# The state's products of a linear-attention layer as two half-width matmuls side by side on TensorE

## The chip, the cores and the metric

The kernel runs on one core of one Trainium2 chip, as one launch. The metric is the device time of that launch in microseconds, taken over several runs. Beside the runs there is one profiled execution with a trace of every instruction. TensorE (PE) does matmuls and, overlapped with them, loads of the stationary operand (PEld); VectorE (DVE), ScalarE (ACT) and GpSimd (POOL) do the elementwise work; SyncE (SP) issues the DMAs.

## The reference

The network is two layers, with the same weights, on x of 2048 tokens by 576 features. Each layer is a linear attention block followed by a block of 64 small experts. The change touches the attention alone:

```python
qkv = (layernorm(x) @ wqkv)          # q, k, v: 32 heads of 18 features
phi = lambda t: jnp.where(t > 0, t + 1, jnp.exp(t)) + 1e-6
pq, pk = phi(q), phi(k)
kv = jnp.einsum("bhsd,bhse->bhde", pk, v)      # the state: 18 x 18 a head, summed over all tokens
z = jnp.einsum("bhsd->bhd", pk)                # the sum of pk over all tokens
num = jnp.einsum("bhqd,bhde->bhqe", pq, kv)
den = jnp.einsum("bhqd,bhd->bhq", pq, z)[..., None] + 1e-6
x = x + (num / den) @ wo                       # heads put side by side again
```

The expert block takes, for each of 32 query heads, the best of 8 keys twice, and adds gelu(x . u[e]) v[e] of the expert that the pair names.

## The kernel before

Tokens are cut into NT = 16 tiles of 128. Each layer has a front over all tiles (transposes `front_T`; k, v and q by `product`; `phi`; then `front_state`), a short stage that turns the state into a folded output matrix (`state_mask`, `state_sum`, `state_fold`), and a back over all tiles (`back_scale`, `back_oT`, `back_out`, then the experts' `exp_...`). Products that need f32 accuracy are made of split operands in f32r, three passes each (`passes`, `product`).

The state is accumulated over the 16 tiles in one PSUM tile, `kva`. `front_state` (lines 275 to 286) makes five f32 matmuls a tile: for each of four chunks of 7 heads, HC = 126 columns, the stationary operand is 126 columns of v and a column of ones, 127 in all, and the moving operand is the same chunk's 126 columns of phi(k); the fifth chunk has 4 heads, 73 by 72. Each product thus holds every pair of heads in its chunk, and only the 18 x 18 blocks on the diagonal are wanted. The row of the ones is the sum z. v is put into `v5` by three ACT copies in `front_v` (lines 244 to 248), two of 252 columns and one of 72, around columns of ones that were set once in `small_loads`.

When the last tile is in, `state_mask` (lines 301 to 308) multiplies the chunks on DVE by a mask of the diagonal blocks into `kvb`, the row of sums included; `state_sum` (line 310) spreads that row over all 128 partitions with five matmuls whose stationary operand `pick` selects it, and ACT copies the result to `zb` (line 317). `state_fold` (line 327) multiplies each chunk's masked block by its rows of wo, which `wo_load` (line 289) loads, and ACT and DVE split the product into `ohi` and `olo` for `back_out`.

The order of the work on PE, ACT, DVE and POOL is written out: `in_order` makes each engine keep the program's order within a block, and the order is given by the loop from line 724 for tiles 2 to 12 of layer 0 (tiles 2 to 9 have the fold of w_q, `fold_mm`, right behind `front_state`), by the strings given to `play`, and by `step2`. In the strings, `st` is `front_state`, `mk` is `state_mask`, `zs` is `state_sum`, `M` is `state_fold`, `wl` is `wo_load`. In layer 0 `mk0.0 zs0.0x2` comes right after `st0.14 st0.15`; in layer 1 the order is `st1.15 mk1.0 M1.1 zs1.0 ...`, and `st1.11 st1.12` are adjacent. SP issues DMAs in the order of the program, each after the waits for its tile.

`fold_mm` (line 542) is the one place where matmuls use a part of the array's columns: the stationary operand has 32 columns, and the output goes to one of four strips of 32 partitions, `p[32 * j:32 * j + 32]`.

Of the kernel before, what the change touches and what calls it, by code (L numbers as in the profile page):

```python
# [11 lines left out]
F32 = mybir.dt.float32  # L12
# [3 lines left out]
AF = mybir.ActivationFunctionType  # L16
ALU = mybir.AluOpType
# [5 lines left out]
P = 128  # L23
NT = S // P
DK, E, NE = 128, 8, 64
HC = 7 * DH
# [9 lines left out]
NB = 5  # L36
# [21 lines left out]
def network(ctx, tc, x_in, wqkv, wo, wq_t, k_t, u_t, v2, c_mask, c_mask4, c_ident, c_code, c_code1, c_scale, c_shift, out):  # L58
    nc = tc.nc

    cp = ctx.enter_context(tc.tile_pool(name="cp", bufs=1))
# [4 lines left out]
    def psum(name):  # L66
        return ps.tile([P, 1024], F32, tag="ps", name=name)

    def halves(t):
        return t.rearrange("p (b c) -> p b c", b=2)[:, :, :HALF]  # L70


    ident = cp.tile([P, P], F32, name="ident")
    mask = cp.tile([HC + 1, HC + 72], F32, name="mask")
    pick = cp.tile([HC + 1, 2 * P], F32, name="pick")
    code_w = cp.tile([P, 512], BF16, name="code_w")
    shift = cp.tile([P, 64], I32, name="shift")
    mhalf = cp.tile([P, 1], F32, name="mhalf")
# [9 lines left out]
    slo = cp.tile([P, 4, 512], F32R, name="slo")  # L88
    vmix = cp.tile([P, D], F32R, name="vmix")

    kvb = cp.tile([HC + 1, 4 * HC + P], F32, name="kvb")
    zb = cp.tile([P, D], F32, name="zb")
    junk = cp.tile([P, D], BF16, name="junk")
    v5 = [cp.tile([P, 4 * (HC + 1) + 73], F32, name=f"v5_{i}") for i in range(2)]

    hl_d = [dr.tile([P, 2, NB, P], F32, name=f"hl_d{t}") for t in range(NT)]
    pq_d = [[dr.tile([P, D], F32, name=f"pq_d{l}_{t}") for t in range(NT)] for l in range(2)]
# [107 lines left out]
    def product(tt, hi, lo, cols, n, cut=HALF, rem=REM, by_block=False):  # L205

        o = psum(f"pp{n}")
        todo = sorted(passes(rem), key=lambda p: p[1]) if by_block else passes(rem)
        for i, (a, b, w) in enumerate(todo):
            wb = hi[:, b] if w == "hi" else lo[:, blocks(rem)[b][1]]  # L210
            for c0, c1, at in ((0, cut, 0), (cut, D, 512)):
                nc.tensor.matmul(o[:, at:at + c1 - c0], tt[a == "lo"][:, b, :], wb[:, cols + c0:cols + c1],  # L212
                                 start=(i == 0), stop=(i == len(todo) - 1))
        return o
# [24 lines left out]
    def front_v(l, t):  # L239
        v = product(tt["f", l, t], whi, wlo, 2 * D, f"v{l}_{t}", cut=2 * HC)  # L240
        yield
        vt = v5[t % 2]
        w = HC + 1
        for c, x in ((0, v[:, :2 * HC]), (2, v[:, 512:512 + 2 * HC])):
            nc.scalar.activation(vt[:, c * w:(c + 2) * w].rearrange("p (c e) -> p c e", c=2)[:, :, :HC],  # L245
                                 x.rearrange("p (c e) -> p c e", c=2), AF.Copy)
        yield
        nc.scalar.activation(vt[:, 4 * w:4 * w + 72], v[:, 512 + 2 * HC:512 + 2 * HC + 72], AF.Copy)

    def front_q(l, t):  # L250
        q = product(tt["f", l, t], whi, wlo, 0, f"q{l}_{t}")
# [23 lines left out]
    def front_state(l, t):  # L275
        fk, vt = tt.pop(("fk", l, t)), v5[t % 2]
        if t == 0:
            kva[l] = psum(f"kva{l}")
        a = kva[l]
        w = HC + 1  # L280

        for c in range(4):
            nc.tensor.matmul(a[:w, c * HC:(c + 1) * HC], vt[:, c * w:(c + 1) * w], fk[:, c * HC:(c + 1) * HC],
                             start=(t == 0 and c == 0), stop=(t == NT - 1), skip_group_check=True)
        nc.tensor.matmul(a[:73, 512:512 + 72], vt[:, 4 * w:4 * w + 73], fk[:, 4 * HC:],
                         start=(t == 0), stop=(t == NT - 1), skip_group_check=True)


    def wo_load(l, t):
        tiles = wob[l] = []  # L290
        for c, tag in enumerate(("x1", "x1", "x1", "x1", "x2")):
            st = wk.tile([P, D], F32, tag=tag, name=f"wob{c}", bufs=BUFS[tag])
            n = HC if c < 4 else 72
            nc.sync.dma_start(st[:n], wo[c * HC:c * HC + n, :])
            tiles.append(st)
        yield

    def chunk(c):
        return slice(c * HC, c * HC + (HC if c < 4 else 72))

    def state_mask(l, t):
        a = kva.pop(l)
        w = HC + 1
        for c in range(4):
            nc.vector.tensor_tensor(kvb[:, chunk(c)], a[:w, c * HC:(c + 1) * HC], mask[:, :HC], op=ALU.mult)
        nc.vector.tensor_tensor(kvb[:73, chunk(4)], a[:73, 512:584], mask[:73, HC:], op=ALU.mult)
        at = chunk(4).start
        nc.vector.tensor_copy(kvb[:72, at + 72:at + P], kvb[:72, at + 16:at + 72])

    def state_sum(l, t):  # L310

        z = psum(f"z{l}")
        for c in range(4):
            nc.tensor.matmul(z[:, 8 + c * HC:8 + (c + 1) * HC], pick[:, :P], kvb[:, chunk(c)], start=True, stop=True)
        nc.tensor.matmul(z[:, 512:584], pick[:73, P:], kvb[:73, chunk(4)], start=True, stop=True)
        yield
        nc.scalar.activation(zb, z[:, 8:584], AF.Copy)

# [8 lines left out]
    def state_fold(l, b):  # L327

        m = psum(f"m{l}_{b}")
        n, c = (HC, HC) if b < 4 else (72, P)  # L330
        for h in range(2):
            nc.tensor.matmul(m[:c, h * 512:h * 512 + HALF], kvb[:n, b * HC:b * HC + c], wob[l][b][:n, h * HALF:(h + 1) * HALF],
                             start=True, stop=True)
        yield

        def part(x, rows):
            return x[rows].rearrange("p (b c) -> p b c", b=2)

        src = halves(m)
        hi, lo = (part(x[:, b], slice(c)) for x in (ohi, olo))  # L340
        nc.scalar.activation(hi, src[:c], AF.Copy)
        if b < 4:
            nc.vector.tensor_tensor(lo, src[:c], hi.bitcast(F32), op=ALU.subtract)
            return

        nc.vector.tensor_tensor(lo[96:112], src[:16], hi[:16].bitcast(F32), op=ALU.subtract)
        nc.vector.tensor_tensor(hi[64:], src[64:], hi[64:].bitcast(F32), op=ALU.subtract)
        nc.scalar.activation(lo[:72], src[:72], AF.Copy)
        nc.scalar.activation(hi[64:72], src[64:72], AF.Copy)
# [246 lines left out]
    def small_loads():  # L596
        for t in v5:
            nc.gpsimd.memset(t, 1.0)
        nc.gpsimd.memset(kpad, 0.0)
        nc.sync.dma_start(kraw, k_t)  # L600
        nc.gpsimd.tensor_tensor(kpad[:, :, 25:32], kraw[:, :, 1:], kraw[:, :, :1].to_broadcast([P, 2, E - 1]),
                                op=ALU.subtract)
        nc.gpsimd.memset(olo[:, 4].bitcast(F32), 0.0)

        nc.gpsimd.memset(mask, 1.0)
        nc.sync.dma_start(mask[:HC, :HC], c_mask[:, 7:])
        nc.sync.dma_start(mask[:72, HC:], c_mask[:72, 7:79])
        nc.gpsimd.tensor_copy(pick[:, :P], ident[:HC + 1, HC:HC + 1].to_broadcast([HC + 1, P]))
        nc.gpsimd.tensor_copy(pick[:, P:], ident[:HC + 1, 72:73].to_broadcast([HC + 1, P]))
        nc.sync.dma_start(code_w, c_code)  # L610
        nc.sync.dma_start(shift, c_shift)

# [43 lines left out]
    keep, rl, lq, ldx, ldq = front_keep, late_load, late_q, back_x, back_pq  # L656
    fl, ln, lv, sv = first_load, first_ln, load_vu, split_vu
    k, v, q, fT, st = front_k, front_v, front_q, front_T, front_state
    wl, mk, zs, M = wo_load, state_mask, state_sum, state_fold
    ld, num, oT, O = back_load, back_scale, back_oT, back_out  # L660
    S, sel, gel, po = exp_scores, exp_select, exp_gelu, exp_out
# [31 lines left out]
    with in_order(*ALL):  # L693
# [17 lines left out]
        first_load(0, 2)  # L711
        wq_in = load_weight(wqkv, 0, REM, "w")
        small_loads()
        first_load(0, 3)
        run(0, (k, 1), (v, 0, 1))
# [135 lines left out]
```

## Time and profile before

| what | value |
|---|---|
| median of 3 runs | 755.47 us (755.28 to 756.19) |
| the profiled execution's own time | 754.99 us |
| its span, first to last instruction | 753.2 us |
| mean granted TensorE clock | 0.999 |
| state matmuls (lines 283 and 285) | 320 records, 37.4 us of PE busy time |

Busy time of a group is the union of its instructions, which overlap their neighbours; a mean duration in ns is that of one instruction from start to end. What a matmul holds PE for is read from the start of one to the start of the next. In a line of the timeline the columns are the start in us, the length in us, the engine, the line of the kernel, the operation, out<-in by the program's names, rows * columns of the array in use, the partitions and elements of the output, and the count.

### The profile page before, as it was taken

Reading aid. Unit: us, or ns where it says so; the run is one execution under the profiler, and the core shown is the slowest. Engines: PE = TensorE matmul, PEld = TensorE weight load, DVE = VectorE, ACT = ScalarE, POOL = GpSimd, SP = SyncE. Lnnn points to the kernel's source line nnn. Section 1 sums busy time; section 2 is a strip of 40 time slices with the busy share of each in tenths; the row PEclk is TensorE's granted clock in tenths of the full one; section 3 lists DMA queues with packets and bytes.
Section 4 is the critical chain, followed back from the end, with each engine's and each line's share of the span. In section 5 each row is a group of like instructions: output and inputs, shape, how many; then the busy total and the mean of one; then the engine's idle time right before and its main releaser. Section 6 shows DMA issues by size and latency. Waiting matters only on the chain. (4 is left out here: it accounts for less than half of the span.)

```text
span 753.2 us, 13998 instructions
## 1 busy us (share of the span) xinstructions
PE 735.4 (98%) x5356; PEld 692.9 (92%) x5356; DVE 459.0 (61%) x1008; ACT 289.0 (38%) x586; POOL 197.1 (26%) x540
## 2 busy tenths in 40 slices
PE   7999999999999999999999999999999999999995
PEld 5999989999998989999999999999999999999984
DVE  5532342324246887666666666464366899899986
ACT  5422232232333544444444444353233333444343
POOL 2110001000002543333333333130033334533431
PEclk9999999999999999999999999999999999999999
DMA  9737446641111322322232212221734323121101
GB/s 272 248 100 243 162 169 220 220 119 49 48 63 32 111 84 82 98 84 83 87 103 105 88 67 76 90 72 51 187 86 118 103 83 114 32 84 44 48 33 63
DMA packets 52267, 79.48 MB, mean 106 GB/s; under 512 B 5480, under 2 KB 22376, under 8 KB 52200
## 3 DMA queue, kind: packets, MB, share of 16 engines
q1 hardware_dynamic: 52200, 78.59, 32.0%
q8 instruction: 42, 0.69, 0.4%
q14 instruction: 25, 0.20, 0.1%
HBM read 55.01 MB, written 23.56 MB: 104 GB/s over the span
## 5 line engine op out<-in xcount | busy, mean ns | idle before, releaser
L219 DVE TENSOR_SCALAR ek<-ek 128x576 f32<-128x576 f32 x32 | 14.7, 459 | 83.6 <-ACT ek L218 83.6
L212 PE MATMUL ppk<-whi,thif 128*128 128x288 f32 x320 | 50.2, 301 | 1.9 <-ACT thif L102 1.9
L402 PE MATMUL ppo<-ohi,thio 126*128 126x288 f32 (+1 forms) x320 | 50.7, 300 | 0.1
L212 PEld LDWEIGHTS ppk<-whi,thif 128*128 128x128 f32 x320 | 44.2, 188 | 5.9 <-issue 3.3
L163 POOL TENSOR_SCALAR rsf<-mvf 128x1 f32<-128x1 f32 x16 | 3.1, 192 | 175.7 <-DVE mvf L161 175.6
L212 PE MATMUL ppk<-whi,tlof 128*128 128x288 f32 x320 | 48.7, 296 | 0.2 <-DVE tlof L103 0.2
L219 DVE TENSOR_SCALAR eq<-eq 128x576 f32<-128x576 f32 x32 | 15.6, 488 | 54.2 <-ACT eq L218 54.2
L212 PE MATMUL ppv<-whi,thif 128*128 128x252 f32 x320 | 48.1, 296 | 0.1
L212 PE MATMUL ppv<-whi,tlof 128*128 128x252 f32 x320 | 47.6, 295 | 0.0
L187 ACT ACTIVATE yb<-x,rsb 128x640 f32<-128x640 f32 x32 | 29.5, 923 | 43.4 <-POOL rsb L180 43.3
L433 PE MATMUL pps<-shi,thib 128*128 128x512 f32 x160 | 44.0, 405 | 1.9 <-ACT thib L102 1.9
L402 PEld LDWEIGHTS ppo<-ohi,thio 126*128 126x128 f32 (+1 forms) x320 | 44.8, 189 | 0.9 <-DVE eq L221 0.3
L212 PEld LDWEIGHTS ppk<-whi,tlof 128*128 128x128 f32 x320 | 44.6, 188 | 0.5 <-DVE tlof L103 0.5
L212 PEld LDWEIGHTS ppv<-whi,tlof 128*128 128x128 f32 x320 | 44.7, 188 | 0.0
L212 PEld LDWEIGHTS ppv<-whi,thif 128*128 128x128 f32 x320 | 44.3, 188 | 0.4 <-ACT thif L102 0.3
L173 ACT ACTIVATE junk<-x,mb 128x576 bf16<-128x576 f32 x32 | 24.7, 771 | 49.7 <-POOL mb L172 46.4
L433 PE MATMUL pps<-shi,tlob 128*128 128x512 f32 x160 | 42.4, 395 | 0.0
L245 ACT ACTIVATE v<-ppv 128x252 f32<-128x252 f32 x64 | 20.9, 380 | 55.0 <-PE ppv L212 55.0
L218 ACT ACTIVATE eq<-ppq 128x576 f32<-128x576 f32 x32 | 20.7, 647 | 52.1 <-PE ppq L212 52.1
L212 PE MATMUL ppq<-whi 128*128 128x288 f32 x260 | 39.9, 300 | 0.6 <-DVE eq L221 0.6
L402 PE MATMUL ppo<-ohi,tloo 126*128 126x288 f32 x256 | 40.3, 295 | 0.0
L402 PE MATMUL ppo<-olo,thio 126*128 126x288 f32 x256 | 40.3, 296 | 0.0
(156 smaller groups left out, 1797.7 us busy)
## 6 DMA issues: line engine op xcount, KB each, us to landing
fold<-in_wq_t SPq DMA_DIRECT2D x64, 288.0 KB, 5.3
whi<-hl_d SPq DMA_DIRECT2D x26, 320.0 KB, 3.9
pq_d<-eq SPq DMA_DIRECT2D x19, 288.0 KB, 2.1
pq<-pq_d SPq DMA_DIRECT2D x19, 288.0 KB, 2.8
xf<-in_x SPq DMA_DIRECT2D x16, 288.0 KB, 5.6
x<-in_x SPq DMA_DIRECT2D x16, 288.0 KB, 2.8
x_d<-x SPq DMA_DIRECT2D x16, 288.0 KB, 3.0
x<-x_d SPq DMA_DIRECT2D x16, 288.0 KB, 2.8
```

The source lines that it names most:

```text
L163: nc.gpsimd.tensor_scalar(rs[:, 0:1], mv[:, 1:2], EPS_LN, 1.0, op0=ALU.add, op1=ALU.mult)
L173: nc.scalar.activation(junk, xt, AF.Square, bias=m[:, 0:1], accum_out=m[:, 1:2])
L187: nc.scalar.activation(y, x2, AF.Identity, scale=rs[:, 0:1], bias=rs[:, 1:2])
L212: nc.tensor.matmul(o[:, at:at + c1 - c0], tt[a == "lo"][:, b, :], wb[:, cols + c0:cols + c1], start=(i == 0), stop=(i == len(todo) - 1))
L218: nc.scalar.activation(e.rearrange("p (b c) -> p b c", b=2), halves(p), AF.Exp)
L219: nc.vector.tensor_scalar(e, e, 1.0, EPS, op0=ALU.min, op1=ALU.add)
L245: nc.scalar.activation(vt[:, c * w:(c + 2) * w].rearrange("p (c e) -> p c e", c=2)[:, :, :HC], x.rearrange("p (c e) -> p c e", c=2), AF.Copy)
L402: nc.tensor.matmul(p[:, h * 512:h * 512 + HALF], hl[a][:r, b], w[:r, h * HALF:(h + 1) * HALF], start=(i == 0), stop=(i == len(todo) - 1))
L433: nc.tensor.matmul(p[:, :512], hl[a == "lo"][:, b, :], shi[:, b] if w == "hi" else slo[:, blocks(REM)[b][1]], start=(i == 0), stop=(i == l ...
```

## The change

The state's products are made in two halves of the array's columns. A chunk of 126 columns of v is cut into two of 63, each with a column of ones (64 stationary columns), and the second half's output goes to partitions 64 to 127 of the same PSUM columns. Each half is multiplied by only those 72 columns of phi(k) that hold its 4 heads: columns 0 to 71 of the chunk for the first half and 54 to 125 for the second. (The middle head lies in both.) The last chunk is cut into two of 36 by 36. So a tile has ten matmuls of 64 stationary and 72 or 36 moving columns in place of five of 127 or 73 by 126 or 72.

The rest follows from the layout: `v5` has ten slots of 64 columns; `kvb` has 128 rows, with a row that is zero at 63 and 127, and is cleared once; wo's rows are loaded in two pieces a chunk; the masks are made by two DVE operations over four chunks each and two for the last chunk; the sums are read from a copy of the state, `zc`, which ACT makes, by four matmuls in place of five; `state_fold` contracts 127 rows (100 for the last chunk) in place of 126 (72).

```diff
-    mask = cp.tile([HC + 1, HC + 72], F32, name="mask")
-    pick = cp.tile([HC + 1, 2 * P], F32, name="pick")
+    mask = cp.tile([P, 72 + 36], F32, name="mask")
+    pick = cp.tile([P, 2, P], F32, name="pick")
+    zc = cp.tile([P, 4 * 72 + 36], F32, name="zc")
...
-    v5 = [cp.tile([P, 4 * (HC + 1) + 73], F32, name=f"v5_{i}") for i in range(2)]
+    v5 = [cp.tile([P, 10, 64], F32, name=f"v5_{i}") for i in range(2)]
...
-        for c, x in ((0, v[:, :2 * HC]), (2, v[:, 512:512 + 2 * HC])):
-            nc.scalar.activation(vt[:, c * w:(c + 2) * w].rearrange("p (c e) -> p c e", c=2)[:, :, :HC],
-                                 x.rearrange("p (c e) -> p c e", c=2), AF.Copy)
-        yield
-        nc.scalar.activation(vt[:, 4 * w:4 * w + 72], v[:, 512 + 2 * HC:512 + 2 * HC + 72], AF.Copy)
+        for c, x in ((0, v[:, :2 * HC]), (4, v[:, 512:512 + 2 * HC])):
+            nc.scalar.activation(vt[:, c:c + 4, :63], x.rearrange("p (c e) -> p c e", c=4), AF.Copy)
+        yield
+        nc.scalar.activation(vt[:, 8:, :36], v[:, 512 + 2 * HC:512 + 2 * HC + 72].rearrange("p (c e) -> p c e", c=2), AF.Copy)
...
-        for c in range(4):
-            nc.tensor.matmul(a[:w, c * HC:(c + 1) * HC], vt[:, c * w:(c + 1) * w], fk[:, c * HC:(c + 1) * HC],
-                             start=(t == 0 and c == 0), stop=(t == NT - 1), skip_group_check=True)
-        nc.tensor.matmul(a[:73, 512:512 + 72], vt[:, 4 * w:4 * w + 73], fk[:, 4 * HC:],
-                         start=(t == 0), stop=(t == NT - 1), skip_group_check=True)
+        for c in range(NB):
+            n, at = (72, 54) if c < 4 else (36, 36)
+            for h in range(2):
+                f0 = c * HC + h * at
+                nc.tensor.matmul(a[64 * h:64 * h + 64, c * 72:c * 72 + n], vt[:, 2 * c + h], fk[:, f0:f0 + n],
+                                 start=(t == 0 and c == 0), stop=(t == NT - 1), skip_group_check=True)
...
-            n = HC if c < 4 else 72
-            nc.sync.dma_start(st[:n], wo[c * HC:c * HC + n, :])
+            r, n = (63, 63) if c < 4 else (36, 36)
+            nc.sync.dma_start(st[:64], wo[c * HC:c * HC + 64, :])
+            nc.sync.dma_start(st[64:64 + n], wo[c * HC + r:c * HC + r + n, :])
...
-        for c in range(4):
-            nc.vector.tensor_tensor(kvb[:, chunk(c)], a[:w, c * HC:(c + 1) * HC], mask[:, :HC], op=ALU.mult)
-        nc.vector.tensor_tensor(kvb[:73, chunk(4)], a[:73, 512:584], mask[:73, HC:], op=ALU.mult)
+        nc.scalar.activation(zc, a[:, :4 * 72 + 36], AF.Copy)
+        for h in range(2):
+            rows = slice(64 * h, 64 * h + 64)
+            nc.vector.tensor_tensor(kvb[rows, :4 * HC].rearrange("p (c e) -> p c e", c=4)[:, :, 54 * h:54 * h + 72],
+                                    a[rows, :4 * 72].rearrange("p (c e) -> p c e", c=4),
+                                    mask[rows, :72].unsqueeze(1).to_broadcast([64, 4, 72]), op=ALU.mult)
         at = chunk(4).start
-        nc.vector.tensor_copy(kvb[:72, at + 72:at + P], kvb[:72, at + 16:at + 72])
+        for h in range(2):
+            rows = slice(64 * h, 64 * h + 64)
+            nc.vector.tensor_tensor(kvb[rows, at + 36 * h:at + 36 * h + 36], a[rows, 4 * 72:4 * 72 + 36], mask[rows, 72:], op=ALU.mult)
+        nc.vector.tensor_copy(kvb[:, at + 72:at + P], kvb[:, at + 16:at + 72])
...
-        for c in range(4):
-            nc.tensor.matmul(z[:, 8 + c * HC:8 + (c + 1) * HC], pick[:, :P], kvb[:, chunk(c)], start=True, stop=True)
-        nc.tensor.matmul(z[:, 512:584], pick[:73, P:], kvb[:73, chunk(4)], start=True, stop=True)
+        zm, sm = (x.rearrange("p (c e) -> p c e", c=4) for x in (z[:, 8:512], zc[:, :4 * 72]))
+        for h in range(2):
+            nc.tensor.matmul(zm[:, :, 72 * h:72 + 54 * h], pick[:, h], sm[:, :, 18 * h:], start=True, stop=True)
+            nc.tensor.matmul(z[:, 512 + 36 * h:548 + 36 * h], pick[:, h], zc[:, 4 * 72:], start=True, stop=True)
...
-        n, c = (HC, HC) if b < 4 else (72, P)
+        n, c = (HC + 1, HC) if b < 4 else (100, P)
...
-        nc.gpsimd.memset(mask, 1.0)
-        nc.sync.dma_start(mask[:HC, :HC], c_mask[:, 7:])
-        nc.sync.dma_start(mask[:72, HC:], c_mask[:72, 7:79])
-        nc.gpsimd.tensor_copy(pick[:, :P], ident[:HC + 1, HC:HC + 1].to_broadcast([HC + 1, P]))
-        nc.gpsimd.tensor_copy(pick[:, P:], ident[:HC + 1, 72:73].to_broadcast([HC + 1, P]))
+        nc.gpsimd.memset(kvb, 0.0)
+        nc.gpsimd.memset(mask, 0.0)
+        nc.sync.dma_start(mask[:63, :72], c_mask[:63, 7:79])
+        nc.sync.dma_start(mask[64:127, :72], c_mask[63:, 61:])
+        for r in (0, 64):
+            nc.sync.dma_start(mask[r:r + 36, 72:], c_mask[:36, 7:43])
+        for h in range(2):
+            nc.gpsimd.tensor_copy(pick[:, h], ident[:, 64 * h + 63:64 * h + 64].to_broadcast([P, P]))
```

More of the change, by code (lines that the diff above doesn't have):

```diff
@@ L89, in network @@
     vmix = cp.tile([P, D], F32R, name="vmix")
-    kvb = cp.tile([HC + 1, 4 * HC + P], F32, name="kvb")
+    kvb = cp.tile([P, 4 * HC + P], F32, name="kvb")
     zb = cp.tile([P, D], F32, name="zb")
     junk = cp.tile([P, D], BF16, name="junk")
-    v5 = [cp.tile([P, 4 * (HC + 1) + 73], F32, name=f"v5_{i}") for i in range(2)]
+    v5 = [cp.tile([P, 10, 64], F32, name=f"v5_{i}") for i in range(2)]
     hl_d = [dr.tile([P, 2, NB, P], F32, name=f"hl_d{t}") for t in range(NT)]
@@ L242, in front_v @@
         vt = v5[t % 2]
-        w = HC + 1
-        for c, x in ((0, v[:, :2 * HC]), (2, v[:, 512:512 + 2 * HC])):
-            nc.scalar.activation(vt[:, c * w:(c + 2) * w].rearrange("p (c e) -> p c e", c=2)[:, :, :HC],
-                                 x.rearrange("p (c e) -> p c e", c=2), AF.Copy)
+        for c, x in ((0, v[:, :2 * HC]), (4, v[:, 512:512 + 2 * HC])):
+            nc.scalar.activation(vt[:, c:c + 4, :63], x.rearrange("p (c e) -> p c e", c=4), AF.Copy)
         yield
-        nc.scalar.activation(vt[:, 4 * w:4 * w + 72], v[:, 512 + 2 * HC:512 + 2 * HC + 72], AF.Copy)
+        nc.scalar.activation(vt[:, 8:, :36], v[:, 512 + 2 * HC:512 + 2 * HC + 72].rearrange("p (c e) -> p c e", c=2), AF.Copy)
     def front_q(l, t):
@@ L279, in front_state @@
         a = kva[l]
-        w = HC + 1
-        for c in range(4):
-            nc.tensor.matmul(a[:w, c * HC:(c + 1) * HC], vt[:, c * w:(c + 1) * w], fk[:, c * HC:(c + 1) * HC],
-                             start=(t == 0 and c == 0), stop=(t == NT - 1), skip_group_check=True)
-        nc.tensor.matmul(a[:73, 512:512 + 72], vt[:, 4 * w:4 * w + 73], fk[:, 4 * HC:],
-                         start=(t == 0), stop=(t == NT - 1), skip_group_check=True)
+        for c in range(NB):
[4 more added lines that the diff above has]
+                                 start=(t == 0 and c == 0), stop=(t == NT - 1), skip_group_check=True)
     def wo_load(l, t):
@@ L302, in state_mask @@
         a = kva.pop(l)
-        w = HC + 1
-        for c in range(4):
-            nc.vector.tensor_tensor(kvb[:, chunk(c)], a[:w, c * HC:(c + 1) * HC], mask[:, :HC], op=ALU.mult)
-        nc.vector.tensor_tensor(kvb[:73, chunk(4)], a[:73, 512:584], mask[:73, HC:], op=ALU.mult)
+        nc.scalar.activation(zc, a[:, :4 * 72 + 36], AF.Copy)
[4 more added lines that the diff above has]
+                                    mask[rows, :72].unsqueeze(1).to_broadcast([64, 4, 72]), op=ALU.mult)
         at = chunk(4).start
-        nc.vector.tensor_copy(kvb[:72, at + 72:at + P], kvb[:72, at + 16:at + 72])
+        for h in range(2):
+            rows = slice(64 * h, 64 * h + 64)
+            nc.vector.tensor_tensor(kvb[rows, at + 36 * h:at + 36 * h + 36], a[rows, 4 * 72:4 * 72 + 36], mask[rows, 72:], op=ALU.mult)
+        nc.vector.tensor_copy(kvb[:, at + 72:at + P], kvb[:, at + 16:at + 72])
     def state_sum(l, t):
         z = psum(f"z{l}")
-        for c in range(4):
-            nc.tensor.matmul(z[:, 8 + c * HC:8 + (c + 1) * HC], pick[:, :P], kvb[:, chunk(c)], start=True, stop=True)
-        nc.tensor.matmul(z[:, 512:584], pick[:73, P:], kvb[:73, chunk(4)], start=True, stop=True)
+        zm, sm = (x.rearrange("p (c e) -> p c e", c=4) for x in (z[:, 8:512], zc[:, :4 * 72]))
+        for h in range(2):
+            nc.tensor.matmul(zm[:, :, 72 * h:72 + 54 * h], pick[:, h], sm[:, :, 18 * h:], start=True, stop=True)
+            nc.tensor.matmul(z[:, 512 + 36 * h:548 + 36 * h], pick[:, h], zc[:, 4 * 72:], start=True, stop=True)
         yield
```

## The prediction

> **What bounds the kernel now.** I read the page first, for the bound.
>
> ```profile
> span 753.2 us, 13998 instructions
> PE 735.4 (98%) x5356; PEld 692.9 (92%) x5356; DVE 459.0 (61%) x1008; ACT 289.0 (38%) x586; POOL 197.1 (26%) x540
> ```
>
> PE (matmuls) is busy for 98% of the span, and no other engine passes 61%. The state's own matmuls lie in two stretches, so the table of windows came next.
>
> ```profile
> core 0: us, PE busy (x) PEld busy (x) DVE busy (x) ACT busy (x) POOL busy (x), PEclk, DMA share, GB/s
> 20.00:230.00 210.00, 209.28 (x1743) 200.12 (x1742) 72.93 (x151) 62.69 (x144) 16.14 (x47) 1.00 0.43 145
> 270.00:540.00 270.00, 268.42 (x1934) 258.05 (x1932) 165.15 (x376) 116.20 (x240) 79.34 (x231) 1.00 0.28 91
> 640.00:753.20 113.20, 104.55 (x662) 94.19 (x660) 99.17 (x244) 45.53 (x91) 42.68 (x122) 0.99 0.15 51
> ```
>
> From 20 to 230 us (layer 0's fronts) and from 270 to 540 us (layer 1's), PE stands idle for 0.7 and 1.6 us in all, at the full clock. The stage without a PE bound, the tail from 640 us, holds no state matmul. So a microsecond taken from the state's place in PE's queue is a microsecond of the span, nearly one for one, and one added is lost the same way. The groups by line, shapes kept apart, give the rates.
>
> ```profile
> L283 PE MATMUL kva<-ek,v 128*127 128x126 f32 x256 | 33.5, 274 | 0.0
> L285 PE MATMUL kva<-ek,v 128*73 128x72 f32 x64 | 9.3, 228 | 0.0
> L283 PEld LDWEIGHTS kva<-ek,v 128*127 128x127 f32 x256 | 31.1, 190 | 0.0
> L285 PEld LDWEIGHTS kva<-ek,v 128*73 128x73 f32 x64 | 8.1, 145 | 0.0
> L550 PEld LDWEIGHTS fold_ps<-fold,kpad 128*32 128x32 f32 x256 | 8.7, 109 | 5.5
> L212 PEld LDWEIGHTS ppv<-whi,tlof 128*128 128x128 f32 x320 | 44.7, 188 | 0.0
> L197 PEld LDWEIGHTS ptb<-ident,yb 128*128 128x128 f32 x160 | 18.8, 140 | 1.9 <-ACT yb L187 1.7
> ```
>
> An f32 matmul of the program makes two records, each a weight load and a matmul: 256 records are 16 tiles, 2 layers, 4 chunks, twice. A duration has a constant part that overlaps the next record; what queues is the part that grows with columns. Matmul: (274 - 228) / (126 - 72) = 0.85 ns per moving column. Load: (190 - 145) / (127 - 73) = 0.83 ns per stationary column. So a record of L283 needs 107 ns of matmul and 105 ns of load, side by side, and one of L285 61 and 61. A load of 128 columns takes 107 ns; a transpose's is 48 ns shorter (140 against 188), 59 ns.
>
> The one place where the kernel already uses part of the array's width is the fold of w_q (L550, 32 columns). The timeline of PE around it, and of PEld at its start, shows all that the sum needs.
>
> ```profile
> 109.94 1.05 PE L283 MATMUL kva<-ek,v 128*127 128x126 f32 x8
> 110.82 0.29 PE L285 MATMUL kva<-ek,v 128*73 128x72 f32 x2
> 111.04 2.18 PE L550 MATMUL fold_ps<-fold,kpad 128*32 128x320 f32 x32
> 113.16 0.40 PE L212 MATMUL ppk<-whi,thif 128*128 128x288 f32 x1
> ...
> 110.88 0.23 PE L285 MATMUL kva<-ek,v 128*73 128x72 f32 x1
> ...
> 112.85 0.38 PE L550 MATMUL fold_ps<-fold,kpad 128*32 128x256 f32 x1
> ...
> 111.04 0.18 PEld L550 LDWEIGHTS fold_ps<-fold,kpad 128*32 128x32 f32 x8
> ```
>
> First, the strips run at the same time: 32 records of 320 or 256 columns would need 16 x 0.27 + 16 x 0.22 = 7.8 us one after another; they take 2.12 us (111.04 to 113.16), 3.7 times less with four strips. Eight loads start within 0.07 us (0.18 less one duration of 0.11), so loads of different strips overlap too. Second, a change of width costs. The last state matmul (110.88) has streamed its 72 columns by 110.94, and the fold's first load starts at 111.04: 0.10 us of nothing, and then a load that nothing hides, 32 x 0.83 = 0.03. On the way out the last matmul (112.85) has streamed 256 columns by 113.07, the next load starts at 113.15, and its 0.107 lies open too: 0.09 + 0.11.
>
> **The change part by part.** *The state's matmuls now.* What a group holds PE for depends on what follows it.
>
> ```profile
> 339.08 1.05 PE L283 MATMUL kva<-ek,v 128*127 128x126 f32 x8
> 339.97 0.29 PE L285 MATMUL kva<-ek,v 128*73 128x72 f32 x2
> 340.10 0.38 PE L197 MATMUL pto<-ident,o 128*128 128x128 f32 x2
> ...
> 311.60 1.05 PE L283 MATMUL kva<-ek,v 128*127 128x126 f32 x8
> 312.48 0.29 PE L285 MATMUL kva<-ek,v 128*73 128x72 f32 x2
> 312.58 0.64 PE L212 MATMUL ppk<-whi,thif 128*128 128x288 f32 x3
> ```
>
> Ahead of transposes: 340.10 - 339.08 = 1.02 us. Ahead of a product: its 128-column load can start only with the last state matmul (312.48 + 0.06) and is done at 312.65, so 1.05 us. Ahead of the fold: 111.04 - 109.94 + 0.03 = 1.13 us. In the order that the code writes out, the 32 tiles make 30 groups: 12 ahead of transposes, 7 of a product, 8 of the fold; two are pairs (one ahead of exp_out's product, 14 and 15 of layer 0 ahead of the mask), and tile 15 of layer 1 stands ahead of its mask.
>
> *The state's matmuls after.* Each half has 10 records a tile: 8 of 72 columns, paced by the matmul at 0.062, and 2 of 36, paced by the load of 64 columns at 0.053: 0.60 us with the second half's offset. Before that 0.10 + 64 x 0.83 = 0.15 for the change of width; behind it 0.09 + 0.06 ahead of transposes, 0.09 + 0.11 ahead of a product. Ahead of the fold it is the old change of width, taken at 0.13, though from 64 columns to 32 no row shows it. What is queued behind the emptied array is the next product or transpose, and ACT, which waits for those. So transposes 1.02 - 0.90 = 0.12 (x12), product 1.05 - 0.95 = 0.10 (x7), fold 1.13 - 0.88 = 0.25 (x8), pair ahead of the product 2.06 - 1.55 = 0.5, pair ahead of the mask 2.03 - 1.35 = 0.7, single ahead of the mask 1.01 - 0.75 = 0.26. Sum: 1.4 + 0.7 + 2.0 + 1.5 = 5.6 us won.
>
> The change of width at 64 columns has no row of its own. From below it is nothing (a half might need no emptied array), from above twice the 0.10 of the fold; I take the fold's, eight times alike. The 0.60 has 0.53 below it (ten loads of 53 ns) and 1.22 above it (twenty records in line, 16 x 0.062 + 4 x 0.055); I take the overlap that the fold shows.
>
> *Mask and sums of z.* Twice a kernel PE waits here.
>
> ```profile
> 228.75 0.88 DVE L305 TENSOR_TENSOR kvb<-kva,mask 127x126 f32<-127x126 f32 x4 [3.77 <-PE kva L285]
> 229.19 1.13 PE L314 MATMUL z<-kvb,pick 127*128 127x126 f32 x8 [0.47 <-DVE kvb L305]
> 230.33 0.70 PE L332 MATMUL m<-wob,kvb 126*126 126x288 f32 x2
> 230.53 0.65 ACT L317 ACTIVATE zb<-z 128x576 f32<-128x576 f32 x1 [3.01 <-PE z L315]
> ...
> 539.62 1.21 PE L332 MATMUL m<-wob,kvb 126*126 126x288 f32 x4 [0.67 <-DVE kvb L305]
> ...
> L305 DVE TENSOR_TENSOR kvb<-kva,mask 127x126 f32<-127x126 f32 x8 | 1.8, 281 | 11.3 <-PE kva L285 11.3
> L306 DVE TENSOR_TENSOR kvb<-kva,mask 73x72 f32<-73x72 f32 x2 | 0.4, 220 | 0.0
> L245 ACT ACTIVATE v<-ppv 128x252 f32<-128x252 f32 x64 | 20.9, 380 | 55.0 <-PE ppv L212 55.0
> L317 ACT ACTIVATE zb<-z 128x576 f32<-128x576 f32 x2 | 1.3, 652 | 6.3 <-PE z L315 6.3
> ```
>
> In layer 0 the z matmuls follow the first mask (0.28). After, they follow ACT's new copy of 324 columns: between 380 ns for 252 and 652 for 576 that is 0.44, 0.16 later. The z matmuls hold 229.19 to 230.33 = 1.14 now; after, at 0.85 ns a column, two records of 288 columns (0.245 each), two of 216 (0.185) and four of 36 behind a 128-column load (0.11): 1.30, 0.16 more. In layer 1 state_fold of chunk 1 comes first; it waits for the second mask, 0.28 + 0.20 into DVE's work, and after for both halves' masks of 288 columns. At (281 - 220) / 54 = 1.13 ns a column one lasts 0.46 and the second starts 0.38 in: 0.84, 0.36 later, and z's 0.16 on top, since zb, ACT's evictions behind it and DVE's olo follow z. Lost: 0.32 + 0.52 = 0.84. It could be nothing, where the next engine's wait absorbs it, or 1.7, were PSUM read slower by ACT and DVE at once.
>
> *At nothing, with its cover.* ACT's copies of v have the same 252 and 72 elements. wo_load has 5 more DMA issues a layer; SP issues the first at 158.3 and the last at 517.9, and PE uses them from 230.33 and 539.62 on. The added waits of PE's sequencer for them lie under running matmuls. state_fold takes 127 or 100 rows for 126 or 72, and rows don't pace (L332's columns are the same).
>
> ```profile
> L294 SPq DMA_DIRECT2D wob<-in_wo x10: 327/367/389, 158.3 to 517.9; - x10
> L603 POOL MEMSET olo<- 128x576 f32 x1 | 0.6, 577 | 0.0
> POOL rsf L163 <- DVE mvf L161: 175.6, 15, 19.9
> ```
>
> Its ten added issues at 0.37 us would be 3.7 us if nothing covered them. POOL's new memset of kvb is about 0.63 us beside L603's 0.577 for 576 columns, where POOL waits for work (175.6 us in 15 waits); two more mask loads on SP stand ahead of loads of x and of the fold; at L294's 0.37 us each they would cost 0.7 us if those were late.
>
> **Sum.** 5.6 - 0.8 = 4.8 us off the profiled execution's 754.99 (the span's 753.2 and 1.8 us around it, which nothing here touches): 750.2. The median of the runs is 0.48 above it, so 750.7.
>
> **The rivals.** *One half after the other (slower).* If loads or matmuls of the two halves take turns, a tile's state takes 20 records in line, 1.22 for 0.60: 32 x 0.62 = 19.8 us more than forecast, 770. It turns to a loss as soon as a tile's records take over 0.60 + 4.8 / 32 = 0.75 us. For it: half-width pairs stand in no row, and their records are four times shorter than the fold's, so a load has 0.062 to hide in and not 0.27. Against: the fold's 3.7 of 4, and its eight loads in 0.07 us. If the halves were not placed as halves at all, the switches go but the line stays: 32 x (1.22 - 1.01) = 6.7 slower, 762. Together 0.12. The Trainium skill's "TensorE: Matmul & The Clock Gate" (Part 3, What overlaps and what doesn't) says that a load overlaps a running matmul only where the row groups differ; both halves use all rows, and by it twenty loads and matmuls would stand in a line, 20 x 0.115 = 2.3 us, 32 x 1.7 = 54 us more than forecast. The trace disagrees already at full width, where 8 records take 0.88 us (109.94 to 110.82) though load and matmul in a line would be 8 x 0.21 = 1.7.
>
> *Half of the overlap.* If two halves give 1.6 and not 2, a tile takes 0.77, 0.17 x 32 = 5.4 more: 756, no change. The fold's 3.7 of 4 speaks against it, its long records for it: 0.07. The same page (Part 3, Measured speedup vs the span model) gives 2.38 for three column strips; taken as 0.79 of the ideal that is the 1.6 here, an estimate from that page, and the fold's row measures 0.92.
>
> *A dearer change of width.* The change adds 30 entries and 20 exits. At twice 0.10 each the gain goes: 755.7. Eight equal rows speak against it; that none is for 64 columns, for it: 0.08. With no wait at all it would be 50 x 0.1 less: 745.7, chance 0.05.
>
> **How the numbers follow.** The forecast has 0.68, with a range of its own of 748 to 753.5 (the bounds on masks and z, and some 0.03 us a group either way). The 8-in-10 range reaches to the dearer change and half overlap above and towards the free change below: 746 to 757. A measurement of this kernel tells 0.2%, 1.5 us, from no change. Faster: 0.68 + 0.05 and a part of the middle cases, 0.76. Same: 0.11. Slower: 0.13, the halves in line and the worst of the middle cases.
>
> **What would show it.** In the profile after: the lines after L283 have 640 records, 20 a tile; 0.60 us from its first matmul to the end of its last; ahead of it and behind it 0.10 us without PE; groups ahead of transposes 0.90, ahead of the fold's first matmul 0.88 with its load. Records spaced at 0.06 in pairs are right, at 0.06 singly wrong. PE's wait ahead of z grows from 0.47 to about 0.6, that ahead of L332 in layer 1 from 0.67 to 1.0. The prediction is wrong if the tail after 540 us changes its length by over 1 us, or if PE waits for ACT's copies of v.

## The result, and the profile after

The changed kernel takes 750.73 us (median of 4 runs, 750.35 to 752.02) against 755.38 us for the kernel before on the same chip (755.13 to 756.19): a ratio of 0.9938, 95% interval 0.9926 to 0.9949. In a later measurement (after_again below) it was 751.17 against 755.65, 0.9939 with 0.9927 to 0.9951. So it is 4.5 to 4.7 us faster; 4.8 was forecast. The profiled execution happens to be the longest of its four runs (752.02); about 1 us of that lies in its first 15 us and is told further down.

The page of the changed kernel opens like this (its headings left out):

```profile
span 750.2 us, 14647 instructions
PE 731.1 (97%) x5672; PEld 681.5 (91%) x5672; DVE 460.1 (61%) x1006; ACT 289.6 (39%) x588; POOL 197.5 (26%) x541
```

PE has more records (5672 for 5356: ten more in each of 32 tiles, four fewer at the sums of z) and less busy time. The table of windows, cut where it was cut before, shows that PE is still busy for nearly all of both stretches of fronts:

```profile
20.00:230.00 210.00, 208.87 (x1921) 196.30 (x1921) 74.84 (x153) 65.06 (x148) 17.45 (x49) 1.00 0.43 146
270.00:540.00 270.00, 267.24 (x2093) 252.52 (x2092) 165.45 (x374) 115.52 (x239) 79.21 (x231) 1.00 0.28 93
640.00:750.20 110.20, 101.74 (x643) 91.66 (x641) 96.89 (x239) 44.69 (x88) 40.49 (x116) 0.99 0.15 52
```

The 0.7 us of idle PE in the first became 1.1 and the 1.6 in the second 2.8; of the 1.2 more in the second, 0.87 are the longer wait ahead of state_fold that is shown below. Where the time went is read best between fixed instructions of the two traces, which leaves the start out (starts in us, differences worked out):

| stretch | before | after | change |
|---|---|---|---|
| first q product to layer 0's last state matmul | 200.13 | 196.45 | -3.68 |
| from there to state_fold's first matmul (mask, z) | 1.84 | 2.14 | +0.30 |
| to layer 1's first state matmul | 70.78 | 70.95 | +0.17 |
| to layer 1's last state matmul | 237.61 | 235.90 | -1.71 |
| to state_fold's first matmul (mask) | 0.90 | 1.77 | +0.87 |
| to the end | 213.56 | 213.57 | 0.0 |
| sum | 724.83 | 720.77 | -4.06 |

The gain lies in the two fronts (not all of it in the state, as shown below), the loss at the two hand-overs, and the rest of the span is shifted and unchanged, the tail included. The trace of after_again has 196.55 and 235.89 for the fronts and 213.77 for the tail, in all 721.05: 3.8 us less than before. So by the traces, without the start, the gain is 3.8 to 4.1 us.

The timeline of PE and PEld around one tile ahead of the fold, the same tile as before:

```profile
109.31 0.49 PE L199 MATMUL ptf<-ident,yf 128*128 128x128 f32 x3
109.73 0.81 PE L286 MATMUL kva<-ek,v 128*64 128x72 f32 x20
110.47 0.77 PE L558 MATMUL fold_ps<-fold,kpad 128*32 128x320 f32 x8
...
109.73 0.70 PEld L286 LDWEIGHTS kva<-ek,v 128*64 128x64 f32 x20 [0.17 <-issue]
```

`128*64` is the half width. Twenty loads and twenty matmuls, and 0.74 us from the first to the fold's first matmul. The first matmul's record begins with its load, so 0.05 for that load, 0.60 for the records and 0.13 for the old change of width, 0.78 in all, had been worked out. The last pair of records starts 0.59 us after the first and streams 36 columns, 0.03: less the load, the twenty records take some 0.56 us. Ahead of them PEld stands 0.17 us with nothing to wait for that the profile shows: the last transpose starts at 109.53 (109.31 and two steps of 0.108), has streamed 0.11 later, and 0.09 us pass before the first load at 109.73.

Ahead of a transpose and ahead of a product the timeline of PE shows:

```profile
336.70 0.86 PE L286 MATMUL kva<-ek,v 128*64 128x72 f32 x20
337.48 0.77 PE L199 MATMUL pto<-ident,o 128*128 128x128 f32 x5
...
309.43 0.81 PE L286 MATMUL kva<-ek,v 128*64 128x72 f32 x20
310.17 0.54 PE L214 MATMUL ppk<-whi,thif 128*128 128x288 f32 x2
```

The product follows 0.74 us after the first state matmul, as the fold did, the transpose 0.78: in the eight steps of this kind the last chunk starts 0.04 us late. It starts 0.06 us after the end of ACT's third copy of v, which full-width matmuls had reached later.

In these eight steps of layer 1 (tiles 2 to 9) another engine holds PE a moment later. `thib` and `tlob` are the two parts into which ACT and DVE split the transposed input of the experts (`ptb`); `pps` is the experts' first product from it. The same step before and after, all engines, only the lines that matter:

```profile
355.72 0.71 PE L197 MATMUL ptb<-ident,yb 128*128 128x128 f32 x5
357.42 0.96 DVE L103 TENSOR_TENSOR tlob<-ptb,thib 128x768 fp32r<-128x768 f32 x1 [0.22 <-ACT thib L102]
357.93 0.71 PE L197 MATMUL pto<-ident,o 128*128 128x128 f32 x5
358.42 0.30 PEld L433 LDWEIGHTS pps<-shi,thib 128*128 128x128 f32 x2
```

```profile
353.15 0.71 PE L199 MATMUL ptb<-ident,yb 128*128 128x128 f32 x5
354.85 0.96 DVE L105 TENSOR_TENSOR tlob<-ptb,thib 128x768 fp32r<-128x768 f32 x1 [0.17 <-ACT thib L104]
355.23 0.77 PE L199 MATMUL pto<-ident,o 128*128 128x128 f32 x5
355.86 0.30 PEld L441 LDWEIGHTS pps<-shi,thib 128*128 128x128 f32 x2
```

The state stands between the first line and the third. It is shorter after, and yet the stretch from the transposes `ptb` to `pps` takes 2.71 us in both (355.72 to 358.43, 353.15 to 355.86). In all eight steps after, and in all before, the load of `pps` starts 0.05 us after DVE's `tlob` has ended, and by its semaphore it waits for that. Before, that wait kept PEld for some 0.03 us (0.07 in one step); after, for 0.10. PE counts as busy meanwhile, with the transposes `pto`, so the table of windows does not show it. From one `pps` to the next a step takes 17.79 us before and 17.75 after: 0.04 gained where 0.12 was forecast. In tile 0's step, a little ahead of these eight, `pps` waits for ACT's `thib` in the same way, and the stretch is 3.01 us before and after.

One more difference lies where nothing was changed. The product that makes v (`ppv`) has the same 28 records a tile as before, and the timeline of PE from its first record to what follows it shows it shorter after than before:

```profile
101.41 1.49 PE L212 MATMUL ppv<-whi,thif 128*128 128x252 f32 x10
105.11 0.71 PE L565 MATMUL fold_pt<-ident,foldf 128*128 128x128 f32 x5
```

```profile
101.18 1.46 PE L214 MATMUL ppv<-whi,thif 128*128 128x252 f32 x10
104.82 0.71 PE L573 MATMUL fold_pt<-ident,foldf 128*128 128x128 f32 x5
```

3.70 us became 3.64. Its records of 324 columns start 149 ns apart before and 146 after, on the mean. From the start of its first record to that of its last a tile takes 3.554 us before (the median of 30 tiles) and 3.496 after, and 3.496 in the trace of every other run here but line65 (3.512). Over 30 tiles that is 1.8 us, nearly half of the gain by the traces, and it lies in other matmuls than the state's; the 0.04 us that the eight steps gained is no more than this. Of this product the change can have moved the place of its operands in SBUF, since tiles set out ahead of them in the kernel have other sizes. That this is the cause is not shown and stays open.

The two hand-overs, all engines, only the lines that matter:

```profile
225.55 0.51 PE L286 MATMUL kva<-ek,v 128*64 128x72 f32 x12
226.11 0.44 ACT L305 ACTIVATE zc<-kva 128x324 f32<-128x324 f32 x1 [0.54 <-PE kva L286]
226.58 0.93 DVE L308 TENSOR_TENSOR kvb<-kva,mask 64x288 f32<-64x288 f32 x2 [3.48 <-ACT zc L305]
226.69 0.72 PE L322 MATMUL z<-zc,pick 128*128 128x288 f32 x2 [0.63 <-ACT zc L305]
227.98 0.73 PE L340 MATMUL m<-wob,kvb 127*126 127x288 f32 x2
...
535.10 0.44 ACT L305 ACTIVATE zc<-kva 128x324 f32<-128x324 f32 x1 [4.57 <-PE kva L286]
535.57 0.92 DVE L308 TENSOR_TENSOR kvb<-kva,mask 64x288 f32<-64x288 f32 x2 [7.52 <-ACT zc L305]
536.60 0.96 PE L340 MATMUL m<-wob,kvb 127*126 127x288 f32 x3 [1.54 <-issue]
```

ACT's copy takes the 0.44 us that were estimated, and z the 1.3 (226.69 to 227.98 is 1.29). But DVE's masks do not start beside the copy: their idle time ends with it (`<-ACT zc L305`), 0.47 us later than the copy's start. In layer 0 z hides that; in layer 1 state_fold waits for the masks and gets it in full.

### The profile page after: what moved, and what is told of

Read it like the earlier page. It is cut to its first block, busy times and chain, and to the rows that moved or that the text cites. A ratio compares the mean times of both kernels' runs of the same rounds, so it can differ in the third digit from the quotient of the medians.

```text
span 750.2 us, 14647 instructions
## 1 busy us (share of the span) xinstructions
PE 731.1 (97%) x5672; PEld 681.5 (91%) x5672; DVE 460.1 (61%) x1006; ACT 289.6 (39%) x588; POOL 197.5 (26%) x541
## 5 line engine op out<-in xcount | busy, mean ns | idle before, releaser
L214 PE MATMUL ppk<-wlo,thif 128*128 128x288 f32 x256 | 40.3, 299 | 0.0
```

## The experiments

The theory: a tile's state is shorter because two half-width strips work at the same time, and what it loses is an emptied array of about 0.1 us and an uncovered load at each change of width. The rivals: the gain is that each matmul streams and loads fewer columns, whether or not the strips overlap; or the change of width is free, or dearer.

### line64: both halves in one strip

The second half's output goes to the same 64 partitions, in other PSUM columns, and is read from there; the work is the same.

```diff
-                nc.tensor.matmul(a[64 * h:64 * h + 64, c * 72:c * 72 + n], vt[:, 2 * c + h], fk[:, f0:f0 + n],
+                nc.tensor.matmul(a[:64, 512 * h + c * 72:512 * h + c * 72 + n], vt[:, 2 * c + h], fk[:, f0:f0 + n],
...
-        nc.scalar.activation(zc, a[:, :4 * 72 + 36], AF.Copy)
+        for h in range(2):
+            nc.scalar.activation(zc[64 * h:64 * h + 64], a[:64, 512 * h:512 * h + 4 * 72 + 36], AF.Copy)
```

> Both halves go to the same strip of 64 array columns (second half to other PSUM columns), so they cannot run side by side; loads, columns and changes of width stay. Theory (the gain is the overlap of two strips): a tile's 20 records take 16 x 0.062 + 4 x 0.055 = 1.21 us for 0.59, 32 x 0.62 = 19.8 us more than the changed kernel, plus about 0.9 us for two more ACT copies of the state: 771 us. Rival (the gain is that fewer columns are streamed and loaded, or the strips took turns already): a tile stays at 0.6 us, 751 to 752 us.

It took 768.29 us (2 runs), 1.0165 of the kernel before (1.0135 to 1.0194). The timeline of PE around a tile ahead of the fold:

```profile
81.10 1.43 PE L286 MATMUL kva<-ek,v 128*64 128x72 f32 x20
82.46 0.50 PE L559 MATMUL fold_ps<-fold,kpad 128*32 128x320 f32 x4
```

1.36 us for 0.74: the 0.62 that a line of twenty records costs. Same records, same loads, same changes of width; only the strip differs. The rival that the fewer columns alone are the gain falls: in line they make the kernel slower than before. (Each matmul streams fewer columns, but the twenty records of a tile together stream 1296 for 1152.) 771 us were expected, 20.7 more than the changed kernel with the two added copies of the state; 17 are seen. About 2 us of what is missing lie in the nine steps of layer 1 where another engine holds PE: eight grow by 0.43 for 0.62 (from 17.75 us to 18.18), since `pps` no longer waits for `tlob`, and tile 0's not at all (3.01 from `ptb` to `pps`).

### line65: in line, at full width

As line64, with 65 columns of v and ones a half, so that the array stays at full width.

```diff
-    v5 = [cp.tile([P, 10, 64], F32, name=f"v5_{i}") for i in range(2)]
+    v5 = [cp.tile([P, 10, 65], F32, name=f"v5_{i}") for i in range(2)]
...
-                nc.tensor.matmul(a[64 * h:64 * h + 64, c * 72:c * 72 + n], vt[:, 2 * c + h], fk[:, f0:f0 + n],
+                nc.tensor.matmul(a[:65, 512 * h + c * 72:512 * h + c * 72 + n], vt[:, 2 * c + h], fk[:, f0:f0 + n],
```

> As line64, but with 65 stationary columns a half, so that the array stays at full width and no change of width is left. Theory: a tile's records in line take 1.22 us, no emptied array ahead and behind: against the kernel before 32 x 0.2 = 6.5 us more, and 1 to 2 us of hand-over: 763 us; and 8 us under line64, which is the price of its changes of width. Rival (a change of width is free or hidden): line65 as slow as line64, within 1 us.

761.65 us (2 runs), 1.0077 of before (1.0048 to 1.0106), and 6.6 us under line64. The timeline of PE:

```profile
80.14 1.38 PE L286 MATMUL kva<-ek,v 128*65 128x72 f32 x20
81.45 0.50 PE L559 MATMUL fold_ps<-fold,kpad 128*32 128x320 f32 x4
```

The mode column reads `128*65`, and the records pace as in line64. What line64 pays on top, 6.6 us over its 30 groups or 0.22 a group, is the changes of width: by the traces a step with the fold is 0.12 longer, where only the way in is new, and each of the eight steps of layer 1 0.29, with the way out. Together the two runs take the result apart: the half sizes without overlap cost 6 us (more than 7 without the shorter v product, which line65 has too), the changes of width 6.6, and the overlap brings 17.

### dummy_mid and dummy_front: the price of a change of width

Both add one full-width f32 matmul of 64 columns a tile into PSUM columns that nothing reads; dummy_mid in the middle of a tile's state, between its second and third chunk (the diff), dummy_front ahead of it, where the array is at full width anyway (the same matmul before the loop over chunks).

```diff
+            if c == 2:
+                nc.tensor.matmul(a[:, 640:704], ident, ident[:, :64], start=True, stop=True, skip_group_check=True)
```

> The changed kernel with one more f32 matmul of 128 x 64, full width, into unused PSUM columns, between chunks 1 and 2 of each tile's state: two more changes of width a tile and the extra work. Theory (an emptied array of 0.095 us at each change, then a load that nothing hides): 0.095 + 0.107 + 0.107 + 0.054 + 0.095 + 0.053 = 0.51 us a tile, 16.4 us: 767. Rival (a dearer change, 0.2 us): 773. Rival (no emptied array): 761.

> The control of dummy_mid: the same matmul ahead of each tile's state, where the array is at full width anyway, so no change of width is added. Theory: two records paced by a 128-column load, 0.21 us a tile, 6.9 us: 757.6, and dummy_mid 9.5 us above it. Rival (a free change): dummy_mid at most 4 us above it.

765.76 us (2 runs) and 754.8 us (8 runs): 11.0 us between them, 0.34 a tile. An emptied array of 0.095 twice and its loads had been put at 9.5, the dearer change at 15 and the free one at 3. The theory's price is right to 0.05 us a tile. The timelines of PE, dummy_mid and then dummy_front:

```profile
344.93 0.47 PE L288 MATMUL kva<-ek,v 128*64 128x72 f32 x8
345.33 0.43 PE L284 MATMUL kva<-ident 128*128 128x64 f32 x2
345.69 0.56 PE L288 MATMUL kva<-ek,v 128*64 128x72 f32 x12
```

```profile
338.88 0.33 PE L282 MATMUL kva<-ident 128*128 128x64 f32 x2
339.15 0.81 PE L287 MATMUL kva<-ek,v 128*64 128x72 f32 x20
339.89 0.55 PE L199 MATMUL pto<-ident,o 128*128 128x128 f32 x3
```

In the middle of a tile's state the two records hold 0.36 us (345.33 to 345.69), and 0.40 pass from the first state matmul to them; at full width ahead of the state they hold 0.27, with the change that was there already. dummy_front itself cost 4 us and not the 6.9 expected. Ahead of the fold it adds 0.17 a tile, since its first load lies under the transposes. In the eight steps of layer 1 it costs nothing: a step takes 17.74 us with it and 17.75 without, because `pps` waits for the end of `tlob` in both. That confirms by experiment that it is not PE that sets the pace there. (The transpose follows 0.74 us after the first state matmul here, not 0.78: the wait for the third copy of v is gone too, and it makes no difference to the step.)

### mask_first: the masks ahead of the copy, in layer 1

```diff
-        nc.scalar.activation(zc, a[:, :4 * 72 + 36], AF.Copy)
+        if l == 0:
+            nc.scalar.activation(zc, a[:, :4 * 72 + 36], AF.Copy)
...
         nc.vector.tensor_copy(kvb[:, at + 72:at + P], kvb[:, at + 16:at + 72])
+        if l == 1:
+            nc.scalar.activation(zc, a[:, :4 * 72 + 36], AF.Copy)
```

> In layer 1 alone ACT's copy of the state stands behind DVE's masks in the program, not ahead of them; layer 0 is as in the changed kernel. Theory (the masks wait for that copy though both only read the state, which costs state_fold 0.46 us in layer 1): PE's wait ahead of state_fold in layer 1 falls from 1.77 to 1.3 us, the sums of z wait a little instead; 0.3 to 0.5 us less than the changed kernel, about what a measurement can tell. Rival (the masks wait for something else, or PSUM is read slower by two engines): DVE's first mask starts no earlier and the time is the same.

751.8 us (5 runs) with a ratio of 0.9947 (0.9933 to 0.9961): in time not to be told from the changed kernel. Its trace is plain, all engines in layer 1's hand-over, only the lines that matter:

```profile
533.90 0.57 PE L286 MATMUL kva<-ek,v 128*64 128x72 f32 x14
534.52 0.92 DVE L309 TENSOR_TENSOR kvb<-kva,mask 64x288 f32<-64x288 f32 x2 [7.04 <-PE kva L286]
535.55 1.21 PE L343 MATMUL m<-wob,kvb 127*126 127x288 f32 x4 [1.07 <-issue]
535.97 0.44 ACT L318 ACTIVATE zc<-kva 128x324 f32<-128x324 f32 x1 [6.02 <-DVE kvb L315]
536.59 0.41 PE L325 MATMUL z<-zc,pick 128*128 128x288 f32 x1
```

The masks now wait for PE alone, and from the last state matmul to state_fold 1.30 us pass instead of 1.77. From the first q product to the end the trace has 719.92 us, for 720.77 and 721.05 in the two traces of the changed kernel, so the 0.47 arrives, and the runs are too far apart to show it. Now ACT's copy waits for the masks (`<-DVE kvb L315`). Both only read the state, yet in both orders the later in the program waits for the earlier. Why stays open.

### pairs, pairs_mask: two tiles' states together

If a change of width costs 0.1 us and a load, two tiles' states behind each other should save it. pairs holds the state of an even tile back to stand ahead of the next one's.

```diff
-                run(0, (q, t), (fT, t + 1), (st, t))
+                run(0, (q, t), (fT, t + 1), (st, t - 1 if t % 2 else -1), (st, t if t % 2 else -1))
...
-        run(1, (v, s - 3), (fT, s - 2), (keep, s - 2 if s - 2 < 13 else -1), (st, s - 3))
+        run(1, (v, s - 3), (fT, s - 2), (keep, s - 2 if s - 2 < 13 else -1), (st, s - 4 if s % 2 == 0 else -1), (st, s - 3 if s % 2 == 0 else -1))
```

> The state matmuls of two neighbouring tiles stand one behind the other for tiles 2 to 11 of layer 0 and 2 to 9 of layer 1: nine entries and five exits from the half width are saved. Theory (0.15 us an entry with its load, 0.15 an exit ahead of transposes): 4 x 0.15 ahead of the fold, 5 x 0.3 elsewhere, 2.1 us less than the changed kernel: 748.6. Rival (the emptied array costs nothing by itself since other engines set the pace there, or the later state holds back tiles of phi(k) and v): 750.7 or more.

> Both edits, pairs and mask_first. Theory: the sum of their gains, 2.5 us less than the changed kernel: 748.2. Rival: no better than pairs alone.

751.98 us (5 runs, ratio 0.9951, 0.9938 to 0.9963) and 751.5 (0.9944, 0.9931 to 0.9956): nothing gained. In layer 0 the trace has the saving: 195.39 us from the first q product to the last state matmul, where the changed kernel had 196.45 and in after_again 196.55. Layer 1 gives it back: 237.70 from first to last state matmul for 235.90. The timeline of pairs in a step of layer 1 without a state, all engines, only the lines that matter:

```profile
353.15 0.71 PE L199 MATMUL ptf<-ident,yf 128*128 128x128 f32 x5
353.35 0.81 ACT L104 ACTIVATE thib<-ptb 128x768 fp32r<-128x768 f32 x1
354.06 0.22 ACT L248 ACTIVATE v<-ppv 128x72 f32<-128x72 f32 x1
354.19 0.96 DVE L105 TENSOR_TENSOR tlob<-ptb,thib 128x768 fp32r<-128x768 f32 x1 [0.17 <-ACT thib L104]
354.33 0.77 PE L199 MATMUL pto<-ident,o 128*128 128x128 f32 x5 [0.48 <-ACT v L248]
355.20 0.30 PEld L441 LDWEIGHTS pps<-shi,thib 128*128 128x128 f32 x2 [0.34 <-DVE tlob L105]
```

Without the state's 0.9 us between the two sets of transposes, the second one (`pto`) stands until ACT has made the third copy of v. That is not the wait that ends last: `pps` then waits 0.34 us more for `tlob`, and the stretch from `ptb` (352.49 us) to `pps` takes 2.71 us, as it did with a state in it. A step with two states takes 3.17. So each of the four pairs of steps loses 0.46 us, 1.8 in all, which is what layer 1 gave back. The state had covered ACT's and DVE's work. The expectation's theory priced the saving rightly and missed the cover; its rival named the loss (other engines set the pace there).

### pairs0_mask and after_again

pairs in layer 0 alone, with mask_first; and the changed kernel beside it.

> The pairs of layer 0 alone (tiles 2 to 11), where the trace of pairs gained 0.85 us, without those of layer 1, where PE then waited 0.64 us for ACT in each step without a state; with mask_first. Theory (an emptied array is paid on PE, and saving it pays where the state covers no other engine's work): 0.85 + 0.47 = 1.3 us less than the changed kernel. Rival (the saving is taken back later, as in pairs): the same as the changed kernel.

> The changed kernel itself, on the same chip as pairs0_mask, so that the two can be compared: 4.8 us under the kernel before by the prediction, 4.6 by the first measurement; if the prediction's parts are right but the first measurement was lucky in the start, 3.5 to 4.5.

750.37 us as the median of five executions (ratio 0.9930, 0.9917 to 0.9943) against 751.17 (0.9939, 0.9927 to 0.9951). A sixth execution took 1827.68 us, which no profile explains; with it the median is 750.49, and the interval leaves it out. By the traces, from the first q product to the end: 719.52 us against 721.05, 1.5 us less where 1.3 was expected; by the runs 0.8 less, with intervals that overlap. pairs0_mask is the best version here by its median, and not proven better than the changed kernel. after_again was expected at 4.8 us under the kernel before by the prediction, or at 3.5 to 4.5 if the first measurement had been lucky: its runs give 4.5, its trace without the start 3.8.

## Why the prediction was right

The time came out as forecast. The pace of the strips, the price of a change of width and the groups where PE sets the pace held; the bound failed in part, one hand-over was mis-sized, and something unforeseen made up for it.

**The bound: the step that failed.** The prediction took PE's 98% and the 0.7 and 1.6 us of idle time to mean that a microsecond taken from the state's place is a microsecond of the span in every group. It was not so in twelve of the 30. In nine groups of layer 1 `ptb` to `pps` takes 2.71 us (3.01 in one) with the long state and with the short one, because ACT's `thib` and DVE's `tlob` end when they did: nothing was won behind `pps`, where 9 x 0.12 = 1.1 us had been forecast. dummy_front and pairs show the same limit from two sides. One product in each layer now waits 0.12 us for ACT's `thif` and wins nothing for 0.10, and the pair ahead of exp_out's product, which then waits for `tlob` too, 0.23 for 0.5. Before the change PE stood at this limit already, with waits of some 0.03 us, and a busy share of 99% could not tell it.

The prediction had said that it would be wrong if PE waited for ACT's copies of v. PE does, 0.04 us in each of the eight steps, but `pps` waits for `tlob` afterwards, so that this wait by itself costs nothing. The state had been work that hid other engines, and the prediction looked for such cover only under the small edits.

**The groups where PE sets the pace.** There the pricing was right. From the start of the instruction ahead of a group to the third record behind it, which counts the load that lies open, 0.27 us were won ahead of the fold for 0.25 forecast, 0.12 ahead of transposes for 0.12, 0.12 ahead of a product for 0.10, and up to the last state matmul 0.7 in the pair ahead of the mask for 0.7 and 0.26 in the single tile for 0.26.

**Overlap and pace.** The step with the most at stake, 0.60 us for twenty half-width records, was taken from the fold's four strips of 32 columns and holds for two of 64 (0.56). line64 measures the other end that was named, 0.62 more a tile. The Trainium skill's page "TensorE: Matmul & The Clock Gate" (Part 3, What overlaps and what doesn't) would have put twenty loads behind twenty matmuls; the runs disagree, at full width (8 records in 0.88 us) and at half width (20 in 0.56).

**The change of width.** It was taken at 0.10 us and a load from eight equal rows at 32 columns. At 64 columns the trace has 0.09; the two dummies give 0.34 a pair of changes with its loads, and line64 against line65 0.12 for a way in and 0.29 for both ways. The Trainium skill's "TensorEngine Tiling (Array Packing)" (Tiling Modes, Key Properties) says that a changed mode drains the engine; the trace agrees, with 0.09 us of nothing ahead of the first load.

**The hand-overs: the term that was mis-sized.** The estimate was 0.32 and 0.52 us. Layer 0's is right: 0.30 in the table, z's 0.16 included. In layer 1, 0.36 were reckoned ahead of state_fold and 0.87 were found. The prediction's bound spoke of PSUM read slower by two engines at once; in fact the engines take turns, and mask_first shows the 0.47 us as a wait for ACT's copy (0.36 and 0.47 make 0.83). On the other side z's 0.16 in layer 1 did not reach the end.

**The sum, and luck.** By the traces the state's groups gave 4.3 us and not 5.6: 3.35 in layer 0 for 3.2, 0.12 in tile 0 (ahead of the table's first stretch) as forecast, and 0.85 in layer 1 for 2.3. The hand-overs took 1.2 for 0.8. So the change as the prediction described it brings 3.1 us, not 4.8. The shorter v product, which stands in no term of the prediction, brought 1.8, and 0.6 went again where the q product waits for DVE, at the start and in two later steps of layer 0. These sums make 4.3 us; the table has 4.2 with tile 0, and after_again 3.9. By the runs, whose start varies (below), it is 4.5 to 4.7. That the median of 750.73 lies 0.03 from the forecast's 750.7 is therefore luck: the groups were taken for too much and the hand-overs for too little, and a gain that the prediction did not foresee made up for most of it.

## What to carry to other kernels

Where f32 matmuls with few moving columns fill the pace of a PE-bound stage, two half-width strips side by side do them in about half the time of a line (0.74 us a tile for 1.36 here). That pays if the group is long enough for the two emptied arrays: here about 0.3 us against 0.6 saved. Price the change of width from any place where the kernel already changes it. Before making PE's work shorter or moving it, look for what that work covers, step by step: PE can be busy for 99% of a stretch and still stand at the limit of another engine in each step of it. Follow from the next product on PE which engine's result it needs last, and compare that time with the state's; a chain like `ptb`, `thib`, `tlob`, `pps` takes the gain back. And compare instructions that the change left alone: here they held 1.8 us that a look at the total would have put down to the state.

## What the runs showed of the hardware

Two strips start together out of the program's order: the program gives two records of the first half, then two of the second, and the trace has the records in pairs 5 to 10 ns apart, one pair every 0.062 us (records of one strip in line64 are 0.062 apart). The fold's four strips start 13 ns apart in the same way.

The start of the kernel is not the same in every execution. The window of 10 to 15 us in the changed kernel's profile, and the same window in after_again, the same program:

```profile
10.00:15.00 5.00, 4.74 (x24) 4.51 (x23) 2.46 (x6) 1.59 (x3) 3.45 (x6) 0.66 1.05 299
```

```profile
10.00:15.00 5.00, 4.74 (x33) 4.16 (x32) 2.62 (x6) 1.82 (x3) 3.45 (x6) 1.00 1.06 335
```

The granted clock (third from the end) was 0.66 in one and 1.00 in the other, and 24 matmuls were done for 33. The first q product came at 29.39 us in the one and at 28.34 in the other. That microsecond is a quarter of the whole effect, and the spread of the runs of most kernels here, 1 to 2 us, is of its size. The mean clocks on record fit it in part: of the 29 executions of the kernel before that were measured beside the experiments, six have a mean clock of 0.996 and five of these are among the nine longest. But the clock falls at the end of the span too (0.51 from 745 us in after_again), and whether the start explains the spread stays open.
